# Who issues the stores of the projection stage: ScalarE or GpSimd

## The chip, the cores and the metric

The kernel runs on one core of a Trainium2 chip. Its time is the device time of one execution in microseconds (us), and the median of several executions is given. The core has five engines with a queue of instructions each, and each queue is worked off in order: TensorE (PE, matmuls and weight loads), VectorE (DVE), ScalarE (ACT), GpSimd (POOL) and SyncE (SP), which here only issues DMAs. An engine waits at an instruction until the semaphores that this instruction names have reached their counts; what stands behind it in the same queue waits too.

## The reference

One transformer block, batch 1, 2048 tokens of width 640, in float32:

```python
x = A_x
h = x + _A_ref(_layernorm(x, axis=-1), A_wqkv, A_wo)            # 32 heads of 20
h2 = h + _B_ref(_layernorm(h, axis=-1), B_w_gate, B_w_up, B_w_down)   # SwiGLU, 1728 wide
```

`_A_ref` multiplies the normalised tokens by `wqkv` (640 x 1920), takes softmax(q k^T / sqrt(20)) v head by head, and multiplies by `wo`. `_B_ref` is (silu(x w_gate) * (x w_up)) w_down. The change touches only the first of these products: queries, keys and values.

## The kernel before, in words

**Stages.** The kernel has three: the projections with the first part of the row maxima (to about 390 us), attention (to about 1580 us), and the output projection with the feed-forward part. The change lies in the first.

**The projection stage.** The 2048 tokens are four chunks of 512 (`c` from 0 to 3). A chunk takes 18 slots (`slot[0] = 18 * c + j`): ten *blocks* (`query_key(c, m)`: 128 rows of transposed queries or keys by 512 tokens, 15 matmuls each) and eight halves of *values* (`value(c, t, half)`: 128 tokens by 320 columns, 15 matmuls each). Every operand is split into a high and a low part (`split`, lines 84 to 86: ACT writes the high part, line 85, and DVE or POOL the difference, line 86), and three products are summed. In the value slots PE also transposes the next chunk's tokens (`flip`, line 417); ACT copies them out (line 283) and splits them.

**What becomes of a block** (`keep`, from line 470 on; chunk 0 has a form of its own). ACT copies the sum from PSUM into one of three buffers `e` (line 494); for key blocks of the first two chunks POOL appends a difference of the two halves (line 496), so that the block is 768 and not 512 wide. Then the *previous* block's stores are issued (`store`, line 435, the DMA in line 438). After the slot's row-maximum work, `finish_keep` splits the block: ACT line 85, POOL line 86. So a block is stored one slot after it was made, in two or three pieces, since a head group has 80 rows and a block 128. Its buffer is written again three blocks later, and that write waits until the stores have landed. Values go from PSUM into one of two tiles `ev` (ACT, line 531), and 128 tokens at a time into `v_d` through the same `store`. `q_d`, `k_d` and `v_d` are tensors in DRAM.

**What reads the stores.** While the projections run, the free time of PE, ACT and DVE is filled with row maxima of the scores, which later stabilise the softmax. `visit(n)` does up to n pairs of them at fixed places of a slot: PE multiplies (line 188), ACT takes one half of the result through a Relu (line 193), DVE adds and reduces (line 195, two instructions a pair). Their operands are pieces of `q_d` and `k_d` that SP has loaded back (`stack`, line 148) into one of five places, four tiles `raw` and one `fifth`. Which piece is loaded and used in which slot is fixed when the program is built. SP also loads the next chunk's tokens (`xt`, line 279).

**What sets the order around the change.** Each engine's queue is the order of the Python calls. SP issues the stores of the slots before the tenth and the last blocks' ones; from the tenth slot on ACT issues them, between its own activations. Each DMA counts its landing on one of eight semaphores that the build hands out in turn, and a DMA waits until the one before it on its semaphore has landed, if that isn't known yet. In the listing of the built program SP and ACT draw from the same eight; a DMA issued by POOL draws from eight others.

```python
        stores = []
        def store(*last, queue=nc.scalar):
            while stores:
                queue.dma_start(*stores.pop(0))
            stores.extend(last)
```

Of the kernel before, what the change touches and what calls it, by code (L numbers as in the profile page):

```python
# [44 lines left out]
def tile_block(ctx: ExitStack, tc: tile.TileContext, x, wqkv, wo, wg, wu, wd, out):  # L45
    nc = tc.nc
# [37 lines left out]
    def split(src, hi, lo, lo_engine=nc.vector):  # L84
        nc.scalar.activation(hi, src, AF.Copy)  # L85
        lo_engine.tensor_tensor(out=lo, in0=src, in1=hi.bitcast(F32), op=ALU.subtract)  # L86
# [179 lines left out]
    def next_e():  # L266
        es.append(es.pop(0))
        return es[-1]

    with tc.tile_pool(name="pa", bufs=2) as pa:  # L270
# [161 lines left out]

        stores = []

        def store(*last, queue=nc.scalar):

            while stores:
                queue.dma_start(*stores.pop(0))
            stores.extend(last)

        def query_key(c, m):

            z_hi, z_lo = zs[c]
            ps = ps_wide()[:, 0, :] if slot[0] < 6 else ps_one()
            for n, (a, w) in enumerate(((z_hi, w_hi), (z_lo, w_hi), (z_hi, w_lo))):
                for k in range(ND):
                    nc.tensor.matmul(  # L447
                        ps, w[:, k, m * P : (m + 1) * P], a[:, k, :],
                        start=(n == 0 and k == 0), stop=(n == 2 and k == ND - 1),
                    )  # L450
                    if n == 1 and k == 3 and c:
                        visit(3)
            keep(c, m, ps)
# [22 lines left out]
        def keep(c, m, ps):  # L476

            e, before = next_e(), halved[:]
            halved.clear()
            which, half, n = 1 - m % 2, CH // 2, CH  # L480
            hi, lo = e[:, 0], e[:, 1]
            copy = lo.bitcast(F32)
            over = copy[:, CH:]
            if slot[0] < 8:
                if which:
                    nc.scalar.activation(over, ps[:, half:], AF.Copy)
                    nc.vector.tensor_tensor(
                        out=over, in0=ps[:, :half], in1=over, op=ALU.subtract
                    )
                split(ps, hi[:, :CH], lo[:, :CH], nc.vector)  # L490
                if which:
                    halved.append(lambda: split(over, hi[:, CH:], lo[:, CH:], nc.gpsimd))
            else:
                nc.scalar.activation(copy[:, :CH], ps, AF.Copy)
                if which and c < 2:
                    nc.gpsimd.tensor_tensor(
                        out=over, in0=copy[:, :half], in1=copy[:, half:CH], op=ALU.subtract
                    )
                    n = EW
                halved.append(lambda n=n: split(copy[:, :n], hi[:, :n], lo[:, :n], nc.gpsimd))  # L500
            for f in before:
                f()
            n = EW if which and c < 2 else CH
            r0 = m // 2 * P
            pieces, r = [], r0
            while r < r0 + P:
                g, i = divmod(r, GD)
                w = min(GD - i, r0 + P - r)
                dst = (q_d, k_d)[which][c][g].bitcast(F32).rearrange("i r c -> r i c")
                pieces.append((dst[i : i + w], e[r - r0 : r - r0 + w, :, :n].bitcast(F32)))  # L510
                r += w
            sync = slot[0] < 10 or (c, m) == (NC - 1, 2 * ND - 1)
            store(*pieces, queue=nc.sync if sync else nc.scalar)

        def value(c, t, half):
            z_hi, z_lo = zs[c]
            ev = evs[t % 2]
            ps = ps_one()[:, :HALF]
            cs = slice(2 * D + half * HALF, 2 * D + (half + 1) * HALF)
            n = 0  # L520
            for a, w in ((z_hi, w_hi), (z_hi, w_lo), (z_lo, w_hi)):
                for k in range(ND):
                    nc.tensor.matmul(  # L523
                        ps, a[:, k, t * P : (t + 1) * P], w[:, k, cs],
                        start=(n == 0), stop=(n == 3 * ND - 1),
                    )
                    n += 1
                    if n == 9 and slot[0] > 9:
                        visit(2)
            dst = ev[:, half * 4 : half * 4 + 4, : G * VW].rearrange("p g (h w) -> p g h w", h=G)  # L530
            nc.scalar.activation(
                dst[:, :, :, :DH], ps.rearrange("p (g h d) -> p g h d", g=4, h=G), AF.Copy
            )
            if half == 1:
                rows = slice((c * TPC + t) * P, (c * TPC + t + 1) * P)
                store((v_d[rows], ev))
            else:
                store()
# [33 lines left out]
        for c in range(NC):  # L572
# [7 lines left out]
            for j, (kind, *which) in enumerate(work):  # L580
# [20 lines left out]
                if which:  # L601
                    if (c, j) == (0, 0):
                        first_blocks((0, 1), (1, 0), (1, 1), (0, 2), (1, 2))
                        for m, ps in enumerate(firsts):
                            keep(0, m, ps)
                    else:
                        (query_key if kind == "block" else value)(c, *which)
# [558 lines left out]
    def quarter_sums(j):  # L1166

        z0, z1 = z2_c[0], z2_c[1]
        r = {}

        def by_tiles(t):
            return t.rearrange("p (t n) -> p t n", t=TPC)

        def back(name, z, q):
            r[name] = tmp()
            z = quarter(z, q)
            nc.vector.tensor_tensor(
                out=by_tiles(r[name]), in0=z[:, :, 0, j].bitcast(F32), in1=z[:, :, 1, j].bitcast(F32),
                op=ALU.add,
            )  # L1180

        def minus(out, a, b):
            nc.gpsimd.tensor_tensor(out=r[out], in0=r[a], in1=r[b], op=ALU.subtract)

        def keep(name, t, q):
            t = quarter(t, q)
            split(by_tiles(r[name]), t[:, :, 0, j], t[:, :, 1, j], nc.vector)

        return [
            lambda: (back("11", z0, 0), back("12", z1, 0)),  # L1190
            lambda: (back("22", z1, 1), back("21", z0, 1), minus("11", "12", "11"),
                     minus("12", "22", "12")),
            lambda: (minus("22", "22", "11"), minus("21", "21", "22"), keep("11", t14, 0)),
            lambda: (keep("12", t32, 0), keep("22", t32, 1), keep("21", t14, 1)),
        ]
# [493 lines left out]
```

## Time and profile before

| what | us |
|---|---|
| time, median of 3 runs | 2099.12 (2096.74 to 2101.63) |
| time of the profiled execution | 2101.44 |
| span of the profiled execution, first to last instruction | 2099.6 |
| projection stage, about | 0 to 390 |
| attention, about | 390 to 1580 |
| output projection and feed-forward part, about | 1580 to 2100 |

The granted TensorE clock is 0.996 of full speed over the span. In the profile a line number such as L438 is a line of the kernel; names such as `k_d<-e` are destination and source of an instruction; "ACTq" and "SPq" are the sequencers of ACT and SP, which issue DMAs. A view of waits names for each idle stretch what ended it; the chain of waits follows from the last instruction back to what released it, step by step.

### The profile page before, as it was taken

The page shows a single profiled execution, that of the slowest core. Times are in us where ns is not written, and L with a number is a line of the kernel's source. Part 1 is how long each engine was busy: PE and PEld are TensorE (multiplying, and loading weights), DVE is VectorE, ACT ScalarE, POOL GpSimd, SP SyncE. Part 2 cuts the span into 40 slices and gives each one's busy share as a digit, 9 for nine tenths or more (in the row PEclk, how much of TensorE's full clock was granted, in tenths as well). Part 3 has the DMA queues.
Part 4 walks back from the last instruction along what each step waited for, and adds up shares of the span by engine and source line. Part 5 has one row for each costly group of instructions (what it writes and reads, how often), then busy time and mean ns, then how long its engine had stood idle before and what let it go on. Part 6 is the DMA issues. An engine that isn't in the chain of part 4 may idle for free.

```text
span 2099.6 us, 37152 instructions
## 1 busy us (share of the span) xinstructions
PE 2062.0 (98%) x12636; PEld 1204.8 (57%) x12636; DVE 1660.0 (79%) x3631; ACT 1444.2 (69%) x2835; POOL 691.7 (33%) x949
## 2 busy tenths in 40 slices
PE   8989999999999999999999999999999999999998
PEld 6656566433334333333333433335578888888888
DVE  7677867788888888888888888887358666666677
ACT  4557575899999999999999999996743222212221
POOL 2221110234343424353420001001145444753555
PEclk9999999999999999999999999999999999999999
DMA  8575543345253443543631213132138755884542
GB/s 261 178 221 169 173 130 124 87 116 150 90 182 106 151 136 118 154 142 128 188 118 57 52 32 95 34 98 79 35 122 277 255 179 180 302 300 158 198 149 93
DMA packets 197285, 305.38 MB, mean 145 GB/s; under 512 B 47440, under 2 KB 82256, under 8 KB 196072
## 3 DMA queue, kind: packets, MB, share of 16 engines
q1 hardware_dynamic: 186168, 280.18, 42.3%
q10 hardware_dynamic: 10928, 22.82, 3.6%
q8 instruction: 102, 1.67, 0.3%
q14 instruction: 87, 0.71, 0.1%
HBM read 203.82 MB, written 98.30 MB: 144 GB/s over the span
## 4 chain that ended last, share of the span: by engine, by line
PE 87%; DVE 5%; DMA 4%; issue 1%; ACT 1%; POOL 1%; SPq 0%; ACTq 0%; DVEq 0%; POOLq 0%
PE acc L991 24%; PE ps_one L981 15%; PE ps_a L1152 14%; PE ps_max L204 12%; PE ps_b L1246 7%; PE ps_one L523 3%; PE ps_one L447 3%; PE ps_wide L188 3%; DVE over L195 2%; PE ps_max L712 2%; PE ps_b L712 1%; DVE mx L180 1%; DMA t<-t_d 1%; PE ps_wide L447 1%; DMA k_d<-e 1%
## 5 line engine op out<-in xcount | busy, mean ns | idle before, releaser
L987 ACT ACTIVATE probs<-ps_one 128x512 f32<-128x512 f32 x2048 | 1056.8, 616 | 62.1 <-PE ps_one L981 37.3
L210 DVE TENSOR_REDUCE mx<-ps_max 128x1 f32<-128x512 f32 x1472 | 925.9, 684 | 108.0 <-PE ps_one L981 77.2
L981 PE MATMUL ps_one<-q_stk,k_stk 62*128 62x512 f32 x2048 | 585.5, 450 | 2.5 <-DVE m L86 1.8
L991 PE MATMUL acc<-probs,v_stk 128*32 128x512 f32 x4096 | 545.1, 604 | 0.0
L981 PEld LDWEIGHTS ps_one<-q_stk,k_stk 62*128 62x128 f32 x2048 | 251.3, 184 | 432.8 <-ACT probs L987 397.4
L204 PE MATMUL ps_max<-k_stk,q_stk 60*128 60x512 f32 x1472 | 381.5, 425 | 0.0
L204 PEld LDWEIGHTS ps_max<-k_stk,q_stk 60*128 60x128 f32 x1472 | 271.6, 186 | 24.0 <-DVE mx L210 1.2
L195 DVE CUSTOM_DVE_ANT_0 over<-ps_wide,over 128x256 f32<-128x256 f32 x512 | 185.5, 420 | 87.1 <-ACT over L193 86.5
L1367 DVE TENSOR_TENSOR tmp<-ps_a,tmp 128x512 f32<-128x512 f32 x208 | 141.3, 689 | 120.4 <-PE ps_a L1152 94.6
L193 ACT ACTIVATE over<-ps_wide 128x512 f32<-128x512 f32 x256 | 139.0, 597 | 90.3 <-PE ps_wide L188 46.1
L1246 PE MATMUL ps_b<-halves,yp 128*128 128x320 f32 x1032 | 179.3, 308 | 1.9 <-DMA halves<-j_d 1.5
L991 PEld LDWEIGHTS acc<-probs,v_stk 128*32 128x32 f32 x4096 | 80.5, 108 | 174.2 <-issue 165.6
L1246 PEld LDWEIGHTS ps_b<-halves,yp 128*128 128x128 f32 x1032 | 165.1, 188 | 18.6 <-POOL yp L86 1.5
L1026 POOL TENSOR_TENSOR o<-o,rb 128x512 f32<-128x512 f32 x31 | 39.9, 1287 | 410.5 <-DMA q_stk<-q_d 146.3
L1152 PE MATMUL ps_a<-t,units 128*128 128x512 f32 x624 | 162.5, 396 | 0.0
L1152 PE MATMUL ps_a<-z,units 128*128 128x512 f32 x516 | 133.8, 394 | 0.0
L1152 PEld LDWEIGHTS ps_a<-t,units 128*128 128x128 f32 x624 | 112.6, 188 | 18.6
L86 POOL TENSOR_TENSOR yp<-y,yp 128x256 fp32r<-128x256 f32 x96 | 60.3, 628 | 187.9 <-ACT yp L85 187.9
L1251 DVE TENSOR_TENSOR h<-ps_b,h 128x320 f32<-128x320 f32 x248 | 110.0, 481 | 6.9 <-PE ps_b L1246 5.4
L1152 PEld LDWEIGHTS ps_a<-z,units 128*128 128x128 f32 x516 | 93.1, 187 | 15.9
L85 ACT ACTIVATE yp<-tmp 128x512 fp32r<-128x512 f32 x40 | 25.3, 632 | 103.2 <-POOL tmp L1239 103.2
L1152 PE MATMUL ps_a<-z,lasts 128*128 128x512 f32 x324 | 92.5, 393 | 0.0
(202 smaller groups left out, 2215.9 us busy)
## 6 DMA issues: line engine op xcount, KB each, us to landing
units<-w_d SPq DMA_DIRECT2D x186, 256.0 KB
w_d<-stage SPq DMA_DIRECT2D x106, 256.0 KB
halves<-j_d SPq DMA_DIRECT2D x70, 320.0 KB
j_d<-stage SPq DMA_DIRECT2D x42, 320.0 KB
k_stk<-k_d SPq DMA_DIRECT2D x64, 160.0 KB
q_stk<-q_d SPq DMA_DIRECT2D x64, 160.0 KB
rb<-r_d SPq DMA_DIRECT2D x32, 256.0 KB
raw<-k_d SPq DMA_DIRECT2D x42, 160.0 KB
```

The source lines that it names most:

```text
L193: nc.scalar.activation(over, ps[:, :, CH // 2 :], AF.Relu)
L195: nc.vector.tensor_tensor_reduce(over[:, b], ps[:, b, : CH // 2], over[:, b], 1.0, LOWEST, ALU.add, ALU.max, mx[:, b, pair, t, kc : kc + 1],)
L204: nc.tensor.matmul(ps, queries[u][rows, pair, t * P : (t + 1) * P], keys[u // NC][rows, pair, kc * CH : (kc + 1) * CH], start=True, stop=True,
L210: nc.vector.tensor_reduce(mxs[u][:, b, pair, t, kc : kc + 1], ps, axis=AX.X, op=ALU.max)
L447: nc.tensor.matmul(ps, w[:, k, m * P : (m + 1) * P], a[:, k, :], start=(n == 0 and k == 0), stop=(n == 2 and k == ND - 1),)
L981: nc.tensor.matmul(ps, keys[u // NC][rows, p, kt * P : (kt + 1) * P], queries[u][rows, p, :], start=True, stop=True,)
L987: nc.scalar.activation(probs[p][:, b, :], ps, AF.Exp, scale=scale)
L991: nc.tensor.matmul(acc[32 * j : 32 * j + 32, :], values[u // NC][:, kt, j * VW : j * VW + 32], probs[j // 2][:, j % 2, :], start=(kt == 0) ...
L1152: nc.tensor.matmul(ps.rearrange("p (t n) -> p t n", t=TPC), w[k][:, i], z[k][:, :, j], start=(first and m == 0), stop=(last and m == len(n ...
L1246: nc.tensor.matmul(ps, a, b, start=(n == 0), stop=(n == len(pairs) - 1))
L1251: nc.vector.tensor_tensor(out=h, in0=ps, in1=h, op=ALU.add)
L1367: add = lambda out, ps, x: nc.vector.tensor_tensor(out=out, in0=ps, in1=x, op=ALU.add)
```

## The change

```diff
-        def store(*last, queue=nc.scalar):
+        def store(*last, queue=nc.gpsimd):
...
             sync = slot[0] < 10 or (c, m) == (NC - 1, 2 * ND - 1)
-            store(*pieces, queue=nc.sync if sync else nc.scalar)
+            store(*pieces, queue=nc.sync if sync else nc.gpsimd)
```

By the listing of the built programs 85 DMAs move from ACT's queue to POOL's: 69 pieces of 29 blocks and 16 tiles of values. PE's, DVE's and SP's instructions and their order stay as they were. On POOL the DMAs stand in the order of the calls, between the splits (line 86) and the differences (line 496); each waits for the split or the copy that it stores. They now count on semaphores of their own, so that SP's DMAs draw from the first eight nearly alone, and their waits change with that: SP's loads of `raw`, `fifth` and `xt` wait for SP's own earlier DMAs and, where they read what a store wrote, for that store.

## The prediction

> **What bounds the kernel now.** I read the page's busy shares and chain first, then a table of windows over the projection stage, the only one that the change touches.
>
> ```profile
> PE 2062.0 (98%) x12636; PEld 1204.8 (57%) x12636; DVE 1660.0 (79%) x3631; ACT 1444.2 (69%) x2835; POOL 691.7 (33%) x949
> ...
> core 0: us, PE busy (x) PEld busy (x) DVE busy (x) ACT busy (x) POOL busy (x), PEclk, DMA share, GB/s
> 56.00:390.00 334.00, 315.55 (x1561) 209.92 (x1559) 241.04 (x1117) 206.62 (x385) 66.14 (x51) 0.98 0.54 163
> ...
> 70.85:76.70 5.85, 3.73 (x26) 2.90 (x24) 1.56 (x10) 1.47 (x4) 0.00 (x0) 1.00 0.81 223
> 76.70:85.00 8.30, 7.00 (x28) 5.18 (x28) 2.93 (x16) 4.71 (x10) 2.55 (x2) 0.59 0.63 216
> 85.00:89.45 4.45, 4.45 (x30) 3.31 (x29) 2.89 (x16) 3.86 (x8) 1.28 (x1) 1.00 0.11 34
> ...
> 103.90:109.89 5.99, 5.80 (x26) 3.85 (x27) 5.08 (x28) 3.99 (x8) 2.58 (x2) 1.00 0.91 297
> 109.89:121.10 11.21, 6.99 (x23) 4.35 (x21) 3.48 (x17) 3.02 (x5) 2.54 (x2) 0.72 0.68 196
> ...
> 77.28:84.10 6.82, 5.52 (x20) 4.43 (x19) 2.74 (x15) 3.51 (x8) 2.55 (x2) 0.50 0.64 220
> 114.83:121.64 6.81, 5.04 (x15) 3.29 (x17) 2.15 (x12) 2.11 (x4) 0.00 (x0) 0.50 0.62 181
> ```
>
> PE is busy 98% of the span, so what counts is PE's lost time. Between 56 and 390 us PE is idle for 334 - 315.6 = 18.5 us, POOL is busy for a fifth. The next rows are single slots: two value slots of 5.85 and 8.30 us stand before one of 4.45, and a key slot of 11.21 us follows one of 5.99. In both places PE first stands still and then runs at a granted clock of 0.50 for 6.8 us. So a stall is paid twice. The stalls, in the timeline and the chain of waits:
>
> ```profile
> 76.03 0.60 ACT L283 ACTIVATE e<-ps_one 128x512 f32<-128x512 f32 x1 [4.35 <-DMA k_d<-e]
> ...
> 76.68 0.66 PE L417 MATMUL ps_one<-ident,xt 128*128 128x128 f32 x4 [2.12 <-ACT e L283]
> ...
> 111.88 0.50 PE L188 MATMUL ps_wide<-raw 60*128 60x512 f32 x1
> ...
> 116.59 1.62 PE L188 MATMUL ps_wide<-raw 60*128 60x512 f32 x5 [4.22 <-DMA raw<-q_d]
> 65.70 4.28 DMA v_d<-ev
> 70.73 5.20 DMA k_d<-e
> ...
> 104.33 7.29 DMA k_d<-v_stk
> 111.63 4.83 DMA raw<-q_d
> ...
> 121.89 6.33 DMA k_d<-e
> ...
> 70.38 0.78 SPq L438 DMA_DIRECT2D k_d<-e  x2
> ...
> 92.15 1.49 SPq L148 DMA_DIRECT2D raw<-k_d  x4
> ...
> 101.09 1.79 SPq L279 DMA_DIRECT2D xt<-in_A_x  x4
> ...
> SPq L438 <- DMA q_d<-v_stk: 6.8, 1, 6.8
> ...
> SPq L148 <- DMA v_d<-ev: 3.4, 1, 3.4
> SPq L279 <- DMA v_d<-ev: 7.4, 1, 7.4
> SPq L148 <- DMA k_d<-v_stk: 7.7, 2, 7.3
> ```
>
> The rows with a start time have it first and the duration behind it; the last four are SP's waits in the stretches 56 to 80 and 93 to 122 us: total, times, longest. The second stall is the clearest: PE stands from 112.4 to 116.6 for a `raw` piece, the last part of whose load SP issued at 111.63, when ACT's store `k_d<-v_stk` landed after 7.29 us. The load reads `q_d`, and the store writes `k_d`. No data passes between them; SP waits because the load draws the semaphore on which that store still counts. So it is with the `xt` loads at 101.09 behind `v_d` (7.4 us of SP's time). The first stall is a chain of the same kind: SP's stores of `q_d` wait 6.8 us for ACT's store of other rows, then a `fifth` load 3.4 us for ACT's `v_d<-ev`, and behind it in SP's queue stands the `k_d<-e` store, issued only at 70.4 and landed at 75.9, before which ACT may not overwrite that buffer (the 4.35 us) and PE gets no transpose.
>
> **The change part by part.** 85 DMAs leave ACT's queue and go to POOL's.
>
> *Waits that go.* With the stores on POOL's semaphores, these DMAs of SP wait for SP's own earlier DMAs alone. In the changed listing the `raw` load waits for the `raw` load issued at 92.15, for the first `q_d` store from POOL (a block of chunk 0, stored long before) and for PE's last use of its place; the `xt` loads in front of it lose their 7.4 us too. The `xt` loads then go out right after 93.6, and I put this load behind them at about 97 and its landing some 5 us later (its 4.83 above), so before 103; PE reads it at 111.9, or 106.6 once the first stall is gone. Next late is then PE itself. For the first stall, SP's `k_d<-e` waits for SP's own stores of about 56 to 58 us (none of ACT's before them any more) and can go out at about 62 instead of 70.4; with its own 5.20 it lands at 67, and ACT wants the buffer at 71.7. So both stalls go, with their half clock: (5.85 - 4.45) + (8.30 - 4.45) = 5.25 us, and 11.21 - 5.99 = 5.22 us. Together 10.5 us, with 0 as the other end if something else is late there.
>
> *ACT's issue time.*
>
> ```profile
> L438 ACTq DMA_DIRECT2D k_d<-e x21: 309/443/695, 110.0 to 323.8; - x21
> ...
> L438 ACTq DMA_DIRECT2D v_d<-ev x16: 326/344/360, 65.7 to 362.3; - x16
> ...
> 210.15 0.84 PE L188 MATMUL ps_wide<-raw 60*128 60x512 f32 x4
> 210.26 0.60 ACT L494 ACTIVATE e<-ps_one 128x512 f32<-128x512 f32 x1 [0.43 <-PE ps_one L447]
> 210.32 1.52 ACTq L438 DMA_DIRECT2D k_d<-e  x3
> 211.97 1.58 ACT L193 ACTIVATE over<-ps_wide 128x512 f32<-128x512 f32 x3 [1.11 <-PE ps_wide L188]
> 213.90 0.82 PE L188 MATMUL ps_wide<-raw 60*128 60x512 f32 x4
> 214.90 0.51 PE L188 MATMUL ps_wide<-raw 60*128 60x512 f32 x2 [0.19 <-DVE mx L195]
> by line: PE ps_one L523 19.1%; PE ps_one L447 16.7%; DVE over L195 16.6%; PE ps_wide L188 16.0%; issue 5.7%; DVE mx L180 3.8%; ACT over L193 3.6%; ACTq L438 2.9%; DMA k_d<-e 2.4%; PE ps_one L417 2.2%; DMA fifth<-q_d 2.0%; DVE xt L401 1.7%;
> ```
>
> One issue holds ACT's sequencer for about 0.44 us (least, median, most in ns; values 0.34). In the slot at 210 us three of them put off the next L193 until 211.97, though PE's first pair was done at 210.99 at the latest, and L494 at 210.86: about 1 us of ACT's time. DVE hangs on L193, and PE's third pair at 214.90 on DVE. (The row names PE, but PE was done by then; it was the issues.) Taken away, PE's own order is late next: it reaches its first two pairs at 213.90 anyway, so the third could come at about 214.4, and PE gains 0.5 us in such a slot. The last row bounds the sum: on the chain between 121.7 and 390 us these issues hold 2.9% of 268.3 us, 7.8 us, and no more than what lies on the chain can be won by shortening them. As in the slot above only 0.5 of the 1 us reaches PE, I take half, 4 us (ends 0 and 7.8).
>
> *What POOL takes on.* The trace has no DMA issued by POOL.
>
> ```profile
> L86 POOL TENSOR_TENSOR e<-e 128x512 fp32r<-128x512 f32 (+1 forms) x19 | 26.1, 1371 | 120.4 <-ACT e L85 104.4 <-DMA k_d<-v_stk 5.6 <-DMA q_d<-e 5.4
> L496 POOL TENSOR_TENSOR e<-e 128x256 f32<-128x256 f32 x3 | 2.2, 736 | 3.9 <-ACT e L494 3.9
> 107.29 1.85 POOL L86 TENSOR_TENSOR e<-e 128x768 fp32r<-128x768 f32 x1 [1.98 <-ACT e L85]
> L401 DVE TENSOR_SCALAR xt<-xt,mv,r_a 128x640 f32<-128x640 f32 x10 | 7.1, 721 | 0.1
> L180 DVE TENSOR_REDUCE mx<-ps_wide 128x2 f32<-128x1024 f32 x27 | 32.9, 1220 | 2.1 <-PE ps_wide L176 2.0
> ```
>
> I bound one issue by ACT's shortest, 0.31 us, and POOL's long split, 1.85, and take POOL's smallest tensor instruction, 0.74. A block has 69/29 = 2.4 pieces. In a key slot of chunk 1 POOL then works 0.74 + 1.85 + 2.4 x 0.74 = 4.4 us of 5.99, in the other block slots 1.3 + 1.8 = 3.1 of some 6.4: nothing is late, and what hides it is POOL's own idle time. Behind an issue on POOL stand the next split, and behind that ACT and the next store. At 1.85 a key slot of chunk 1 takes 7.0 us, and five of them cost 5 us; the other slots still hold (1.3 + 4.4 = 5.7). So 0, with 5 us as the bad end. A store has time: it went out a slot after its block was made, lands in 4.3 to 7.3 us by the chain's rows, and its buffer is written again two slots after the issue, about 12 us. For most query blocks the store even follows the split directly on POOL, where ACT first had the next block's L494 in front. SP's loads that do read a store wait for it as before.
>
> By the Trainium skill, "DMA: Bandwidth & Descriptors", section "Latency and other measured facts", a DMA from GpSimd has its first byte after about 1 us, one from SP or ACT after 0.6; by that each store would land some 0.4 us later, and the sum would not move, by the 12 us above. No row here shows it.
>
> *Sum*, against the profiled execution (span 2099.6, time 2101.44): 2101.4 - 10.5 - 4 + 0 = 2086.9. The median of the runs is 2.3 us below that execution, so 2084.6 us. Attention starts that much earlier; its PE order is unchanged.
>
> **Rivals.** *POOL jams or one stall stays.* The key slots of chunk 1 lose the 5 us, or one of the two stalls has a second cause close behind. For it: DMA share is 0.91 in the slot before the second stall, so loads may land late anyway. Against: by the estimate above the load lands 3.6 us before its use. Time: 2084.6 + 5 = about 2090, to 2095 with ACT's gain missing.
>
> *Descriptor writing is locked out by DVE.* Each POOL issue would wait for the DVE instruction under way, up to the 1.22 us of L180, and DVE is busy 241 of 334 us. At a mean of 0.4 us of waiting the issue is 1.1, at worst 1.96: at worst 7.3 us of work in a key slot of chunk 1, 1.3 too much in five: 2085 to 2091. Against it: L401 takes 721 ns for 640 elements, 1.13 ns each, L180 1.19: no DVE row here runs at a double rate. The rule is the Trainium skill's, "SBUF — State Buffer", section "SBUF: two separate sides": DVE in a two-port mode shuts GpSimd out from writing descriptors, and it advises the ACT or SP queue.
>
> *Nothing is won.* The waits shown are replaced by true ones (SP now reaches loads of `k_d` sooner and waits for the store there), and DVE's path takes ACT's gain: within 4 us, 2095 to 2103. Against: the two rows that stall PE read nothing of those stores.
>
> *Slower.* One POOL issue is long. It decides from (6.4 - 1.3)/2.4 = 2.1 us an issue on, where POOL becomes the bound of every block slot. At 3 us: the 24 slots outside chunk 1's keys cost 1.3 + 7.2 - 6.4 = 2.1 each, five key slots 2.6 + 7.2 - 6.0 = 3.8 each, 69 us less 14.5: about 2154; break-even is at about 2.2 us. For it: an issue in software has no row here. Against: 2.2 us is above POOL's longest split of a block.
>
> That the change doesn't do what it says is excluded by the listing: 85 DMAs stand in POOL's queue.
>
> **How the numbers follow.** Forecast, both stalls gone (2077 to 2090, by ACT's ends of 0 and 7.8): 0.62, with the lock-out inside it or just beside it: 0.06. A jam or one stall left (2090 to 2095): 0.10. Nothing won (2095 to 2103): 0.08. Slower: 0.14. This kernel's measurement can tell about 0.2%, 4.2 us, from no change; so faster 0.78, same 0.08, slower 0.14. The range 2077 to 2097 holds the forecast, the lock-out, the jam and a part of the fourth case, about 0.8.
>
> **What would show it.** Right: the slots at 70 and 110 us take 4.5 and 6 us, the clock stays at 1.00 there, SP has no wait for `v_d<-ev` or `k_d<-v_stk` before `xt` and `raw`; ACT's L193 follows L494 at once; 85 DMAs on POOL of below 1.4 us each. Wrong: POOL issues above 2 us; ACT's L494 or L85 waiting for a store or for POOL; a half-clock stretch at a new place.

## The result and the profile after

| | before | changed |
|---|---|---|
| median of 4 runs, us | 2100.38 (2096.74 to 2102.32) | 2085.47 (2082.67 to 2086.06) |
| ratio, 95% interval | | 0.9929 (0.9916 to 0.9942) |
| profiled execution: time, span | 2101.44, 2099.6 | 2082.67, 2080.9 |
| granted clock over the span | 0.996 | 1.000 |

The kernel became 14.9 us faster, 0.7% and clear of the noise; its median of 2085.47 us stands against a forecast of 2084.6 us. The profiled execution of the changed kernel is the fastest of its four and that of before was slower than its median, so the two spans differ by more, 18.7 us. From the page of the changed kernel, and from its table of windows over the same slots (columns as before: stretch, length, busy time of PE, PEld, DVE, ACT and POOL, granted clock, DMA share, GB/s):

```profile
PE 2054.1 (99%) x12636; PEld 1201.4 (58%) x12636; DVE 1659.7 (80%) x3631; ACT 1443.0 (69%) x2835; POOL 740.4 (36%) x1034
...
q0 software_dynamic: 6096, 22.81, 3.5%
```

```profile
56.00:376.00 320.00, 311.92 (x1587) 207.87 (x1589) 244.11 (x1121) 209.00 (x392) 118.68 (x137) 1.00 0.56 172
...
70.85:74.40 3.55, 3.55 (x25) 2.98 (x25) 2.05 (x13) 3.02 (x6) 1.50 (x2) 1.00 0.54 194
74.40:79.10 4.70, 4.61 (x28) 3.26 (x26) 2.28 (x13) 3.41 (x7) 1.56 (x2) 1.00 0.69 233
...
98.07:104.06 5.99, 5.79 (x26) 3.84 (x27) 5.07 (x28) 3.91 (x7) 3.72 (x4) 1.00 0.73 214
104.06:108.66 4.60, 4.60 (x23) 2.96 (x21) 2.74 (x14) 3.02 (x6) 3.90 (x5) 1.00 0.67 175
```

The value slots that took 5.85 and 8.30 us take 3.55 and 4.70, the key slot of 11.21 us takes 4.60, and the clock is 1.00 in all of them. POOL's busy time rose by 49 us over the whole span. Next come SP's issues in the timeline of the changed kernel, and then POOL's issues by line (least, median and most in ns):

```profile
63.78 0.97 SPq L438 DMA_DIRECT2D k_d<-e  x2
...
86.80 2.04 SPq L279 DMA_DIRECT2D xt<-in_A_x  x4
93.30 1.44 SPq L148 DMA_DIRECT2D raw<-q_d  x4
94.78 1.73 SPq L148 DMA_DIRECT2D raw<-k_d  x4
102.47 2.71 SPq L148 DMA_DIRECT2D raw<-q_d  x4
```

```profile
L438 POOL DMA_DIRECT2D k_d<-e x21: 510/612/636, 105.4 to 305.8; - x21
...
L438 POOL DMA_DIRECT2D v_d<-ev x16: 540/558/579, 62.2 to 340.0; - x16
L438 POOL DMA_DIRECT2D q_d<-v_stk x12: 510/623/752, 55.9 to 246.0; - x12
...
DMA to landing us min/median/max: 2.2/4.7/7.5
```

The load `raw<-q_d` whose last part went out at 111.63 us is issued at 93.30 in one go, and PE reads it at 106.05 without a wait. A store holds POOL for 0.51 to 0.75 us. The semaphores in the trace bear out the listing: in the kernel before, SP's and ACT's DMAs of this stage count on the same eight, and the store issued at 104.33 us and the load at 111.63 us count on one and the same; in the changed kernel POOL's 85 stores count on eight others.

To see where the 17.6 us before attention came from, three stretches are taken in every kernel below. **S1**: from ACT's third copy of values (line 531) to its eighth, around the first stall. **S2**: from ACT's second copy of a key block of chunk 1 (line 494) to the fourth, around the second. **S3**: from there to attention's first matmul on `probs` (line 991). All are read from the start times in the trace of one execution, in us. The ratio of an experiment is to executions of the kernel before that were taken beside it; their medians lie between 2098.04 and 2100.24 us, so that medians of different rows can be compared to about 2 us only.

| kernel | median | ratio to before (95%) | S1 | S2 | S3 |
|---|---|---|---|---|---|
| before | 2100.38 | | 27.45 | 17.21 | 268.21 |
| changed | 2085.47 | 0.9929 (0.9916 to 0.9942) | 21.65 | 10.59 | 263.00 |
| 1: POOL up to slot 22 | 2090.50 | 0.9958 (0.9945 to 0.9971) | 21.68 | 10.58 | 270.94 |
| 2: POOL from slot 22 on | 2094.51 | 0.9981 (0.9971 to 0.9991) | 28.75 | 15.86 | 263.26 |
| 3: ACT kept busy | 2092.76 | 0.9971 (0.9960 to 0.9983) | 21.66 | 10.57 | 271.36 |
| 4: SP issues all | 2085.38 | 0.9941 (0.9927 to 0.9955) | 22.05 | 10.52 | 263.13 |
| 5: two stores on POOL | 2095.38 | 0.9978 (0.9968 to 0.9988) | 23.20 | 10.59 | 269.08 |
| 6: POOL 1.6 us a store | 2088.89 | 0.9948 (0.9933 to 0.9962) | 21.66 | 10.55 | 268.05 |
| 7: POOL 2.6 us a store | 2127.75 | 1.0126 (1.0108 to 1.0144) | 21.66 | 11.75 | 304.89 |
| 8: all stores on POOL | 2090.94 | 0.9956 (0.9943 to 0.9970) | 21.67 | 10.56 | 263.36 |
| 9: two given back to ACT | 2085.11 | 0.9939 (0.9925 to 0.9952) | 21.69 | 11.38 | 263.24 |
| 10: three given back to ACT | 2089.19 | 0.9958 (0.9944 to 0.9972) | 21.66 | 12.68 | 263.27 |

Before to changed: S1 5.8, S2 6.6, S3 5.2 us. The first two are the stalls with their half clock. The third I put down to ACT's issue time: by the starts of ACT's copies most of it comes in the block slots, 0.3 to 1.0 us in each of eleven, and little in the slots of values, and PE waits for no DMA in S3, before or after.

### The profile page after: what moved, and what is told of

It is laid out like the page before. It is cut to its first block, busy times and chain, and to the rows that moved or that the text cites. A ratio compares the mean times of both kernels' runs of the same rounds, so it can differ in the third digit from the quotient of the medians.

```text
span 2080.9 us, 37196 instructions
## 1 busy us (share of the span) xinstructions
PE 2054.1 (99%) x12636; PEld 1201.4 (58%) x12636; DVE 1659.7 (80%) x3631; ACT 1443.0 (69%) x2835; POOL 740.4 (36%) x1034
## 3 DMA queue, kind: packets, MB, share of 16 engines
q8 instruction: 102, 1.67, 0.3%
## 4 chain that ended last, share of the span: by engine, by line
PE 85%; DVE 5%; issue 3%; DMA 3%; POOL 2%; ACT 1%; SPq 1%; DVEq 0%; ACTq 0%; POOLq 0%
PE acc L991 23%; PE ps_a L1152 15%; PE ps_one L981 15%; PE ps_max L204 11%; PE ps_b L1246 8%; PE ps_one L523 3%; PE ps_wide L188 3%; PE ps_one L447 2%; DVE over L195 2%; PE ps_max L712 2%; DVE mx L180 1%; PE ps_b L712 1%; DMA halves<-j_d 1%; PE ps_wide L447 1%; POOL stage L800 1%
## 5 line engine op out<-in xcount | busy, mean ns | idle before, releaser
L1152 PEld LDWEIGHTS ps_a<-t,units 128*128 128x128 f32 x624 | 112.5, 188 | 18.7
```

Source lines behind the costliest of these rows:

```text
L1152: nc.tensor.matmul(ps.rearrange("p (t n) -> p t n", t=TPC), w[k][:, i], z[k][:, :, j], start=(first and m == 0), stop=(last and m == len(n ...
```

## The experiments

Theory A: the stalls are SP's waits for ACT's stores on a shared semaphore. Rival B: all that counts is that ACT is rid of 85 issues. In every kernel below PE, DVE, ACT and POOL do the same computing in the same order as in the changed kernel; only the DMAs' places and the scratch instructions that are named differ. Line numbers are a few higher where lines were added.

**1 and 2: the change in two halves**

```diff
-        def store(*last, queue=nc.gpsimd):
+        def store(*last, queue=None):
+            queue = queue or (nc.gpsimd if slot[0] < 22 else nc.scalar)
...
-            store(*pieces, queue=nc.sync if sync else nc.gpsimd)
+            store(*pieces, queue=nc.sync if sync else None)
```

The second kernel has `nc.scalar if slot[0] < 22 else nc.gpsimd`.

> Only the 13 stores issued in slots 10 to 21 (up to about 115 us) are on POOL; the other 72 are on ACT as before. Theory A (most of the gain is the two stalls, which end because SP's DMAs no longer wait for ACT's stores on a shared semaphore): both stalls gone, -12.4 us against the kernel before (5.8 + 6.6), so about 2088, the slots at 70 and 105 us as in the changed kernel and no half-clock stretch there. Rival B (the gain is ACT's freed issue time, spread over all 85 stores): 13/85 of 15 us, -2.3 us, about 2098.

> The complement: the 13 stores of slots 10 to 21 on ACT as before, the 72 later ones on POOL. Theory A: both stalls and both half-clock stretches are there as before, only ACT's term is won, 4 to 5 us: about 2096 (-4 to -5). Rival B: 72/85 of 15 us, -12.6 us, about 2088.

With 13 stores on POOL, S1 and S2 are those of the changed kernel to 0.03 us: both stalls are gone. With the other 72 there, both stalls are back (28.75 and 15.86) and S3 is the changed kernel's: ACT's term alone is won, 2094.5 us. So the gain has two parts that add up, as theory A has it: 9.0 and 5.0 us against the executions of before beside them. The first kernel's 2090.5 us is 2.5 above the 2088 expected. S3 shows why: it is 2.7 us longer than in the kernel before, and one slot alone has 2.9 us too much (132.41 - 124.84 = 7.57 us for a slot that takes 4.64). SP's waits between 100 and 150 us in the first kernel, and its timeline:

```profile
SPq L148 <- DMA k_d<-v_stk: 10.9, 3, 9.9
```

```profile
117.28 2.23 SPq L148 DMA_DIRECT2D fifth<-k_d  x4
119.61 4.43 SPq L148 DMA_DIRECT2D raw<-q_d  x4
...
129.14 0.71 PE L188 MATMUL ps_wide<-fifth,raw 60*128 60x512 f32 x3 [0.42 <-DMA raw<-q_d]
```

This `fifth` load is issued at 111.00 in the changed kernel. Here it waits for the first of the stores that ACT issues again (at 114.33), and a new stall of the old kind arises, with 3.41 us of half clock from 130.18 on: the wait moved to where the stores of ACT begin.

**3: ACT kept busy**

```diff
+        pad = evp.tile([P, 320], mybir.dt.bfloat16, name="pad", bufs=1)
...
                 queue.dma_start(*stores.pop(0))
+                if queue is nc.gpsimd:
+                    nc.scalar.activation(pad, pad, AF.Copy)
```

> The changed kernel, but for each store that POOL issues ACT makes one activation of 128x320 on a scratch tile, which holds it for some 0.4 us as its own issue did (0.31 to 0.44 us). No semaphore changes. Theory A: the stalls stay away and ACT's term is lost: +4 to +6 us against the changed kernel, about 2090 to 2091 (-9 to -11 against before). Rival B: all of the gain is given back, 2098 to 2102.

```profile
L442 ACT ACTIVATE pad<-pad x85: 460/463/473, 57.7 to 374.0; 128x320 bf16<-128x320 bf16 x85
```

The 85 activations hold ACT for 39 us, slightly more than the 37 us of its own issues. S1 and S2 do not move (21.66 and 10.57), S3 grows by 8.4 us, and the median is 7.3 us above the changed kernel's. The expected 4 to 6 us were too few, and why an activation costs more in S3 than an issue (8.4 against 5.2 us) is not shown. But the split holds: ACT's time works on S3 alone, and the stalls have nothing to do with it. Rival B, which wants all 15 us back, is out.

**4: SP issues them all**

```diff
-        def store(*last, queue=nc.gpsimd):
+        def store(*last, queue=nc.sync):
...
-            store(*pieces, queue=nc.sync if sync else nc.gpsimd)
+            store(*pieces, queue=nc.sync)
```

> All stores are issued by SP; ACT and POOL issue none in this stage. ACT is as free as in the changed kernel, but the stores count on the same eight semaphores as SP's loads and stand in SP's own queue ahead of them. Theory A: ACT's 5 us are won, but loads wait for stores again, and now also for the split that a store in front of them waits for: the stalls come back or grow, 2094 to 2110. Rival B (all that counts is that ACT is rid of them): as the changed kernel, 2085.

Theory A missed here: 2085.4 us, the same as with POOL and the number that rival B gives, though SP's loads and stores count on the same eight semaphores as before. Since experiments 1 to 3 exclude rival B, it is theory A that wants mending. The timeline of this kernel:

```profile
88.43 3.29 SPq L279 DMA_DIRECT2D xt<-in_A_x  x4
92.41 0.33 SPq L438 DMA_DIRECT2D v_d<-ev  x1
94.98 1.43 SPq L148 DMA_DIRECT2D raw<-q_d  x4
...
100.44 0.80 SPq L438 DMA_DIRECT2D k_d<-v_stk  x2
104.14 1.41 SPq L148 DMA_DIRECT2D raw<-q_d  x4
```

In one queue, the DMA that a load waits for has always been issued before it, so only the rest of its transfer is waited for. In the kernel before, the `xt` load waited for the last `v_d` store of chunk 0, which stood in *ACT's* queue behind a copy that ACT made only at 98.71 us; the listing of the built program has that store eight DMAs ahead of the load, as if ACT had been as far as SP. So theory A has to be narrowed: not the sharing costs time, but a wait across two queues of which the other is late. Neither POOL nor semaphores of POOL's own are needed for the gain.

**5, 9, 10: two and three stores**

In the listing, DMA n of SP and ACT waits for DMA n - 8. Around the second stall that gives two waits across queues: the first `xt` load waits for the last `v_d` store, and the third and fourth part of the `raw` load that PE needs wait for the two pieces of the first key block, `k_d<-v_stk`. Experiment 5 is the kernel *before* with those two pieces on POOL; then the `raw` load's parts wait for SP's own DMAs, and one `xt` load still waits for `v_d`.

```diff
+            if slot[0] == 19:
+                store(queue=nc.gpsimd)
             sync = slot[0] < 10 or (c, m) == (NC - 1, 2 * ND - 1)
```

Experiment 9 is the *changed* kernel with the same lines and `nc.scalar`; experiment 10 has `slot[0] in (18, 19)` and so gives the last `v_d` store back as well.

> The kernel before, with two of the 85 stores on POOL: the two pieces of the first key block of chunk 1 (k_d<-v_stk at 104 us), on which the raw load of the second stall waits. By the listing that load's parts then wait for SP's own DMAs only; the next pair of loads waits for ACT's stores at 110 us and lands close to its use. Theory A: the second stall and its half clock go or shrink to at most 2 us, the first stays: -4.6 to -6.6 us, about 2093 to 2095. Rival B (ACT's freed issue time): 2/85 of 15 us, -0.4 us, 2099.

> The changed kernel with two of its 85 stores given back to ACT: the same two pieces k_d<-v_stk as in the run with two on POOL. By the listing the third part of the raw load that PE first reads at 106.05 us then waits for ACT's store again, which ACT can issue at about 98.1 us and which lands 4.7 to 7.3 us later, at 103 to 105.5; the part lands some 5 us behind that, 108 to 110.5. Theory A: PE stands 2 to 4.5 us there, with up to 3.4 us more at half clock: +2 to +7 us against the changed kernel, 2087.5 to 2092.5, and nothing moves anywhere else. Rival B (ACT's freed issue time): +0.4 us.

> The changed kernel with three stores given back to ACT: the two k_d<-v_stk pieces as before and the last v_d<-ev of chunk 0, which ACT issues at about 93.2 us. By the listing the first xt load then waits for that v_d store, as in the kernel before, and the third part of the raw load, behind the xt loads in SP's queue, for the first k_d piece. If the second stall needs both waits (the xt loads late and beside the k_d store, so that it lands slowly): xt issued at 95 to 98, the k_d store lands 5 to 7.3 us after 98.5, the raw part lands at 108 to 111 where PE needs it at 106: a stall of 2 to 5 us with up to 3.4 us at half clock, +2 to +8 us against the changed kernel, 2087.5 to 2093. If the two k_d pieces alone were enough and landed fast by chance in the run before: a stall in that case as well as in the repeat. If neither: 2085 as there.

SP's waits and timeline around the place, in the kernels of 5, 9 and 10 in this order:

```profile
SPq L279 <- DMA v_d<-ev: 6.9, 1, 6.9
```

```profile
90.38 8.69 SPq L279 DMA_DIRECT2D xt<-in_A_x  x4
99.16 1.67 SPq L148 DMA_DIRECT2D raw<-q_d  x4
```

```profile
SPq L148 <- DMA k_d<-v_stk: 8.4, 2, 7.9
```

```profile
87.37 4.22 SPq L279 DMA_DIRECT2D xt<-in_A_x  x4
93.69 9.32 SPq L148 DMA_DIRECT2D raw<-q_d  x4
```

```profile
SPq L279 <- DMA v_d<-ev: 8.5, 1, 8.5
SPq L148 <- DMA k_d<-v_stk: 6.9, 1, 6.9
```

```profile
94.89 1.79 SPq L279 DMA_DIRECT2D xt<-in_A_x  x4
96.79 8.24 SPq L148 DMA_DIRECT2D raw<-q_d  x4
...
107.76 0.53 PEld L188 LDWEIGHTS ps_wide<-raw 60*128 60x128 f32 x5 [1.92 <-DMA raw<-q_d]
```

These are four cases of two waits. Only the `xt` wait (5): S2 is 10.59, no stall. Only the wait for `k_d` (9): SP waits 7.9 us for it, as long as before (7.3), yet S2 grows by only 0.8 us and the median (2085.11) does not differ from the changed kernel's: my forecast of +2 to +7 us missed, and the +0.4 us of rival B was nearer. Even the 0.8 us are not SP's wait, since PE waits for no DMA in that slot. The second of the two stores held ACT's queue for 1.85 us (why so long is not shown), and ACT's next activation came 2.45 us after the copy that opens the slot, against 1.01 us in experiment 10. In the timeline of experiment 9:

```profile
98.53 2.26 ACTq L438 DMA_DIRECT2D k_d<-v_stk  x2
100.92 1.57 ACT L193 ACTIVATE over<-ps_wide 128x512 f32<-128x512 f32 x3 [1.85 <-issue]
```

The first of the two stores, issued at 98.53, let the load go on at 102.27, so it landed after less than 3.8 us and not the 4.7 to 7.3 that I took, and the load still had 4.26 us before its first use. Both waits (10): the `xt` loads go out eight microseconds later, the last part of the `raw` load is issued only at about 105.0, 0.6 us ahead of the first use of that tile, PE's weight load waits 1.9 us for it, S2 is 12.68, and the median is 3.7 us above the changed kernel's. With all stores on ACT (before), SP is later still (last part at 111.63) and S2 is 17.21. So moving two of 85 stores is enough to end the second stall, and of these cases only those with both waits have it. That the `xt` loads beside the store slowed its landing (7.29 us before, under 3.8 in experiment 9) fits, but was not tried alone.

Experiment 5's median, 4.9 us below before, is not S2's 6.6 alone. Its S3 has a new wait of 1.7 us in one slot (7.64 us from 121.74 on, 5.98 in the changed kernel), from its timeline:

```profile
122.94 1.95 ACTq L438 DMA_DIRECT2D k_d<-e  x2
125.01 1.57 ACT L193 ACTIVATE over<-ps_wide 128x512 f32<-128x512 f32 x3 [2.67 <-DMA k_stk<-k_d]
```

Here ACT itself waits: its second store stands until a load of SP on the same semaphore has landed, though the store writes other rows than that load reads, and ACT's activations stand behind the store. So the wait across queues works both ways. In S3 of the kernel before, ACT's stores at 138.90 and 329.38 us stand for 0.7 and 0.5 us in the same way, behind SP's loads of `raw` and `fifth`, so that a part of S3's 5.2 us may be such waits and not issue time; no run separates the two.

The S1 of experiment 5 shows a small first stall. The stores around S1 are on ACT in three of the kernels, before, 2 and 5, and their traces have 27.45, 28.75 and 23.20 us there, so the size of that stall is not a fixed number. It ends whenever the 13 stores of slots 10 to 21 leave ACT (1) or SP issues them (4); no run moves only the stores that SP waits for there.

**6 and 7: how long a store may hold POOL**

```diff
+        pad = evp.tile([P, 184], F32, name="pad", bufs=1)
...
                 queue.dma_start(*stores.pop(0))
+                if queue is nc.gpsimd:
+                    for _ in range(2):     # 4 in experiment 7
+                        nc.gpsimd.tensor_tensor(out=pad, in0=pad, in1=pad, op=ALU.subtract)
```

> The changed kernel with two tensor instructions of 128x184 on a scratch tile behind each store on POOL, so that one store holds POOL for about 0.6 + 2 x 0.6 = 1.8 us. By the prediction's formula the five key slots of chunk 1 cost up to 1 us each and the others nothing: 0 to +5 us against the changed kernel, 2085 to 2091. If POOL's time were already near its limit in many slots: +20 us or more.

> The same with four such instructions, about 3.0 us a store. The slower rival's formula: 24 slots of 2 us and five of 4 us too much, +50 to +70 us against the changed kernel, 2135 to 2155, so slower than before. If blocks may lag by a slot behind the values' slots without cost: under +20 us.

The rows by line of experiment 7, and POOL's timeline in a key slot of chunk 1:

```profile
L443 POOL TENSOR_TENSOR pad<-pad 128x184 f32<-128x184 f32 x324 | 163.0, 503 | 20.5
...
L440 POOL DMA_DIRECT2D k_d<-e x21 | 12.4, 593 | 2.1 <-POOL e L86 2.1
```

```profile
116.56 1.83 POOL L86 TENSOR_TENSOR e<-e 128x768 fp32r<-128x768 f32 x1
118.36 0.73 POOL L501 TENSOR_TENSOR v_stk<-v_stk 128x256 f32<-128x256 f32 x1
119.04 0.63 POOL L440 DMA_DIRECT2D k_d<-e  x1
119.69 2.22 POOL L443 TENSOR_TENSOR pad<-pad 128x184 f32<-128x184 f32 x4
121.86 0.62 POOL L440 DMA_DIRECT2D k_d<-e  x1
122.50 2.23 POOL L443 TENSOR_TENSOR pad<-pad 128x184 f32<-128x184 f32 x4
```

A scratch instruction took 0.50 us, not the 0.6 taken, so a store holds POOL for 0.59 + 1.0 = 1.6 and 0.59 + 2.0 = 2.6 us. By the slower rival's formula that is 5 x (2.6 + 2.4 x 1.6 - 6.0) = 2.2 us, and 24 x (1.3 + 2.4 x 2.6 - 6.4) + 5 x (2.6 + 2.4 x 2.6 - 6.0) = 27 + 14 = 41.6 us. Measured against the changed kernel: +3.4 and +42.3 us (in the traces S3 is 5.1 and 41.9 us longer). The sum of experiment 7 fits, but in part by luck, since the places do not. By the starts of ACT's copies some 18 us arise in chunk 1's blocks and 3 in chunk 2's, where the formula has 20 and 11, and none in chunk 3's, where it has the rest. The value slots, for which the formula has nothing and in which POOL splits the flipped tokens, have 6 us in chunk 1 and 11 in chunk 2. So a POOL issue is free here because it takes 0.6 us: at 1.6 it costs about a quarter of the gain, at 2.6 the kernel is slower than before.

**8: the remaining stores on POOL too**

```diff
-            sync = slot[0] < 10 or (c, m) == (NC - 1, 2 * ND - 1)
-            store(*pieces, queue=nc.sync if sync else nc.gpsimd)
+            store(*pieces)
...
-        store(queue=nc.sync)
+        store()
```

> The changed kernel with the stores that SP still issues (slots before the tenth and the last block's) on POOL too; SP then only loads. SP's loads land earlier, but PE waits for none of them: within 1.5 us of the changed kernel, 2084 to 2087. If SP's stores still delay loads that PE waits for: -2 to -4 us.

This missed: 2090.9 us, 5.5 above the changed kernel. S1, S2 and S3 are the changed kernel's to 0.4 us, so the loss lies before S1, in the first ten slots: ACT's first copy of values comes at 62.40 us instead of 56.40. The timeline of this kernel, and then that of the changed one:

```profile
36.03 4.50 SPq L148 DMA_DIRECT2D q_stk<-q_d  x4
...
46.74 1.19 PE L176 MATMUL ps_wide<-k_stk,q_stk 60*128 60x512 f32 x3 [1.76 <-DMA q_stk<-q_d]
```

```profile
36.76 1.46 SPq L148 DMA_DIRECT2D q_stk<-q_d  x4
...
43.17 0.85 PE L176 MATMUL ps_wide<-k_stk,q_stk 60*128 60x512 f32 x4
```

PE waits for the first queries that are loaded back, and a stretch of half clock (6.83 us from 45.8 on) begins there. The stores that POOL issues from 31.0 to 33.5 us land 8.8 to 9.8 us later there. Why they and the load are slow, an earlier start beside the weights' loads or the new order of waits, was not separated.

## Why the prediction was right

**The two stalls, 10.5 us forecast: 12.4 in the trace.** The mechanism was as put: SP's `k_d<-e` stores went out at 63.78 (forecast about 62), the `raw` load at 93.30 (forecast about 97), and both half-clock stretches are gone. The size was off in the second: I took 5.99 us as the slot's undisturbed length, from the slot before it, but that slot has more row-maximum work (DVE is busy 5.07 us in it and 2.74 in the next), and undisturbed the stalled one takes 4.60. The experiments narrow the reason. Semaphores of POOL's own are one way to end the waits, not the only one; experiment 4 ends them with one queue. And "both stalls go" was safer than I argued for the second stall: either of SP's two waits alone makes no stall (5 and 9). The 12.4 us rest on one trace of each kernel, and the first stall's share of them is one draw, since S1 differs by up to 5.6 us between kernels with the same stores on ACT there.

**ACT's issue time, 4 us forecast: 5.2 in the trace**, and experiment 2, which has only this part of the gain, is 0.0019 faster (0.0009 to 0.0029), 1.9 to 6.1 us. The halving was an estimate from one slot; of the 7.8 us on the chain two thirds were won. That it is all issue time is not shown (see experiment 5 on ACT's own waits). As forecast, line 193 now follows line 494 at once, from the timeline of the changed kernel, in the slot that stood at 210 us before:

```profile
194.80 1.66 POOL L438 DMA_DIRECT2D k_d<-e  x3 [0.30 <-POOL e L86]
...
196.70 0.60 ACT L494 ACTIVATE e<-ps_one 128x512 f32<-128x512 f32 x1 [0.40 <-PE ps_one L447]
...
197.19 1.65 ACT L193 ACTIVATE over<-ps_wide 128x512 f32<-128x512 f32 x3
```

By the Trainium skill, "DMA: Bandwidth & Descriptors", section "Issuing engines are not separate DMA queues", starting DMAs from several engines saves only the issuing sequencer's time. Here that part is at most 5.2 of 17.6 us; the larger part comes from waits that the build hangs on the queues, so that in this kernel the change saved more than the section names.

**What POOL takes on, 0 forecast: 0 measured.** Experiment 4, in which POOL issues none of the stores, has the changed kernel's median (2085.38 against 2085.47) and its S3 (263.13 against 263.00). The issue was taken at 0.74 us and is 0.51 to 0.75. The lower bound, 0.31, was ACT's; the upper, 1.85, lies between experiments 6 and 7 (+3.4 us at 1.6, +42 at 2.6), so it might have cost more than the 5 us that I gave it.

**The sum.** The terms of the trace give 17.6 us before attention where I had 14.5; the medians differ by 14.9. The four executions of each lie 3.4 and 5.6 us apart, and the profiled ones were a slow one of before and the fastest of after, so that the median is nearer to my sum than the trace is. That the forecast of 2084.6 us came within 1 us is in part luck.

**The rivals.** *One stall stays* and *nothing won*: no, SP's waits for ACT's stores have no successor that PE sees; in the changed kernel PE waits for no DMA from 56 us to the start of attention.

*DVE locks out descriptor writing*: it happens, but rarely, and it is short. Five of POOL's 85 issues begin while line 401 runs on DVE. They are the five longest, 0.667 to 0.752 us, and each ends 0.10 to 0.18 us after line 401 does; beside all other work of DVE, which is busy 244 of 320 us, the other 80 take 0.51 to 0.65 us. It is not the store that makes the difference: in experiment 6 two of the same five go out shortly before line 401 begins, and take 0.54 and 0.62 us. From the timeline of the changed kernel:

```profile
145.23 1.27 POOL L86 TENSOR_TENSOR v_stk<-v_stk 128x512 fp32r<-128x512 f32 x1 [3.19 <-ACT v_stk L85]
145.71 1.66 DVE L401 TENSOR_SCALAR xt<-xt,mv,r_a 128x640 f32<-128x640 f32 x2
146.80 1.30 POOL L438 DMA_DIRECT2D q_d<-v_stk  x2 [0.30 <-POOL v_stk L86]
```

The same rows show that my argument against this rival misread a mean. The 721 ns of line 401 mix eight instructions of 0.60 to 0.62 us with two of 1.13 and 1.23 us. These two begin while a split of POOL runs and end 0.35 us after it, in the kernel before as in the changed one, where the first of the two shown lasts 1.14 us. So line 401 needs at most 0.35 us for its 640 elements once POOL is done, 0.55 ns each, about half of the 1.19 ns of line 180: a row of a double rate was there. By the Trainium skill, "SBUF — State Buffer", section "SBUF: two separate sides", DVE in a two-port mode shuts GpSimd out from writing descriptors; the trace agrees, if line 401 runs in such a mode, and puts the price at some 0.1 us in five of 85 issues, which POOL's idle time hides.

*Slower*: its condition, an issue of 2.1 us or more, was not met; experiment 7 shows that a store of 2.6 us makes the kernel slower, by about the formula's total but not in its places.

## What to carry to other kernels

When a DMA waits for another one whose data it does not touch, look at which queue holds that other one: a wait in the same queue costs the rest of a transfer, a wait for a queue that is behind costs the whole lag. Moving the few stores concerned to a queue that is not behind ends it: moving 13 of 85 ended both stalls here, and SP served as well as POOL. Look at both sides, for the queue that is behind may also be held by a DMA of the other. Before a store goes to an engine that also computes, multiply its issue time by the stores of its fullest slot.

## What the runs showed that was not expected

- A store that SP waits 7.9 us for can cost nothing: the loads are issued some 11 us ahead of their use (94.74 to 106.05 in the changed kernel), and only what goes beyond that reaches PE (experiment 9). A store that takes 1.85 us to issue cost more, 0.8 us, through ACT.
- Stalls of the same kind cost very different times, the more so where a half-clock stretch follows: S1 has 5.8 us more than in the changed kernel with one of 6.83 us at 77.28 (before, PE's wait for ACT 2.12 us), 7.1 us with one of 10.24 us (experiment 2), and 1.6 us without (experiment 5, PE's wait 1.30 us). All such stretches before the end of the span are about 3.41, 6.83 or 10.24 us long.
- Experiments 5, 8 and 10 show a half-clock stretch of 3.41 us at 373 to 380 us, where attention begins, experiment 7 one of 6.83 us at 412 us, and the profiled execution of the changed kernel none. Its three other runs are 2.6 to 3.4 us slower, two of them with a mean clock of 0.999 and one with 1.000; whether they have such a stretch is not shown.
- POOL issues a store of 16 to 128 rows in 0.51 to 0.75 us; ACT took 0.31 to 0.82 for all but one of its 85, and 1.67 for that one. POOL's stores land 2.2 to 7.5 us later, much as ACT's did (4.3 to 7.3 on the chain).
